# Order of VectorE's queue in the first batch of a Fourier and mixer kernel: weight sums first, two folds spread over more quarters

## The chip, the cores and the metric

The kernel runs on one core of one Trainium2 chip. The metric is the device time of one execution in microseconds (us). A difference of one to three us in 607 is at stake, so beside the times I use the traces: one profiled execution of each kernel, in which the start of every instruction can be read.

Engines: PE is TensorE (matmuls), PEld its weight loads, DVE is VectorE, ACT is ScalarE, POOL is GpSimd, SP is SyncE. In these traces VectorE works through its queue in the order in which the program issued its instructions; when the first one waits, those behind it wait too, ready or not (3.67 us of it are shown below).

## The reference, cut to what matters

```python
X = np.fft.fft(np.fft.fft(x, axis=1), axis=2)     # x: 8 batches of 3008 x 256
x = X.real
h  = np.maximum(x.transpose(0, 2, 1) @ w_tok1, 0) @ w_tok2
u  = x + h.transpose(0, 2, 1)
h2 = np.maximum(u @ w_ch1, 0) @ w_ch2
return u + h2
```

The real part of a two-dimensional Fourier transform of each batch is followed by a token mixer and a channel mixer.

## The kernel before: the parts that the change and the argument touch

The batches are pipelined. While batch b runs through its two channel products (`mm1`, `mm2`), pieces of the front part of batch b + 1 (transform and token mixer) and of the *fold* of batch b + 2 are strewn between them. x1 is the input of batch 1, fold one its fold, and so on. A batch has 24 *quarters* (`sub`): six columns of 512 tokens (`c`) in four steps (`s`). The fold is VectorE work: it adds mirrored rows, which a gather has brought into `xm`, to the rows in `xp`, and writes sums and differences of mirrored channels to `eo`. It has four groups of three pieces:

```python
def fold(b, engs):
    xp, xm = x_tiles.pop(b)
    eo = perb.tile([KR, NR, D], FP16, tag="eo", name="eo")
    for s, (t0, t1) in enumerate(((13, 17), (9, 13), (5, 9), (1, 5))):
        ...
        tt(out=xp[:, t, 1:D], in0=xp[:, t, 1:D], in1=xm[0:KR, rv, D - 1:0:-1], op=add)   # L457
        yield
        tt(out=eo[:, t, 1:129], in0=xp[:, t, 1:129], in1=xp[:, t, 255:127:-1], op=add)   # L461
        yield
        tt(out=eo[:, t, 129:256], ..., op=sub)                                           # L463
        yield
```

`xp`, `xm` and `eo` have one buffer each, so the load of x2 can start only when the last piece of fold one has read x1.

The second channel product takes seven block products in place of eight. It needs four sums of its weights once (`weight_sums`, L233 in the trace, read in batch 0 from quarter 9 on) and, for every column, sums of blocks of the activations (`block_sums`, L753):

```python
def weight_sums():                     # wc2 -> wst, four VectorE adds
    ...
def block_sums(c1, sb, k, which):      # c1 -> sb and in place in c1, VectorE
    ...
def mm2_sums(b, c, c1, s, box):        # per quarter: 24 small matmuls (L777) that read c1, sb, wc2, wst
    ...
    # L762 on VectorE and GpSimd: adds that empty PSUM into the output tile osb
```

The main loop of before, cut to the schedule:

```python
plan = [[0] * 10 + [2] * 14,  [1] * 13 + [0] + [2, 1] * 5]     # pieces of the front part of b + 1
fold_at = [15, 10]
for b in range(BB):
    nxt = front(b + 1) ...
    folds = fold(b + 2, ...)
    for c in range(NCH):
        for s in range(4):
            sub = 4 * c + s
            n = plan[b > 0][sub]
            mm1(b, c, c1, range(3 * s, 3 * s + 3))
            if s == 3: now()                  # block_sums
            take(own, ...); take(nxt, n // 2)
            if s == 0: now()
            mm2(*prev, s, pbox)
            if s == 2: now()
            ...
            take(nxt, n - n // 2)
            if s == 1: now()
            ...
            if b == 0 and sub == 4:
                weight_sums()
            if b == 0 and sub == 3:
                for h in range(2): swap_wc1(h)
            if b == 0 and 3 <= sub < 9:
                take(early, 2)                # early = fold(1)
                if sub == 8: x_tiles[2] = load_x(2)
            if folds is not None and sub >= fold_at[b > 0]:
                take(folds, 1 + (b == 0))
                ...                           # load_x(b + 3) after the last piece
```

## Time and profile before

| | before |
|---|---|
| time, median of 3 (lowest to highest) | 607.27 us (607.20 to 607.56) |
| span in the profile | 605.8 us |
| TensorE busy | 97% |
| listed TensorE waits in batch 0 (46 to 112 us) | 3.1 us |
| listed TensorE waits after 112 us | none |

From the page of before: busy time of each engine, and the shares of the chain of waits by engine.

```profile
PE 589.6 (97%) x6323; PEld 421.7 (70%) x6323; DVE 454.3 (75%) x1022; ACT 437.0 (72%) x983; POOL 148.5 (25%) x234
...
PE 86%; DMA 6%; DVE 5%; issue 1%; ACT 1%; POOL 1%; DVEq 0%; POOLq 0%
```

The list of TensorE's waits of before in 46 to 112 us (total, times, longest):

```profile
PE py L777 <- DVE sb L753: 1.7, 2, 1.2
PE pt L604 <- DVE w L590: 0.7, 1, 0.7
PE px L777 <- DVE osb L762: 0.5, 2, 0.2
PE px L777 <- DVE c L753: 0.2, 1, 0.2
```

Here `sb` and `c` are the block sums, `osb` is the output tile, and `w` is what the front part's transform hands to its token product (L604). From 46 us on TensorE is the limit, and all that it waits for is VectorE, in the first batch. Why VectorE is late shows in its timeline (start, duration, instruction, idle time before it and its releaser):

```profile
41.33 0.68 DVE L704 TENSOR_TENSOR ut<-pu,yt 128x512 f16<-128x512 f32 x1
45.68 0.23 DVE L455 TENSOR_TENSOR xp<-xp,xm 94x16 f16<-94x16 f16 x1 [3.67 <-DMA xm<-in_x_dram,ix]
...
47.12 0.68 DVE L704 TENSOR_TENSOR ut<-pu,yt 128x512 f16<-128x512 f32 x1
47.71 1.01 DVE L233 TENSOR_TENSOR wst<-wc 128x768 f16<-128x768 f16 x2
...
58.58 0.54 DVE L753 TENSOR_TENSOR sb<-c 128x768 f16<-128x768 f16 x1
59.16 0.56 DVE L753 TENSOR_TENSOR sb<-sb,c 128x768 f16<-128x768 f16 x1
...
80.60 1.21 DVE L455 TENSOR_TENSOR xp<-xp,xm 94x16 f16<-94x16 f16 x1
```

VectorE stops 3.67 us at the first piece of fold one, because the gather of x1 has not landed. The weight sums and an add for u (L704) stand behind that piece and could have run. From 45.7 us on VectorE works without a break, and the block sums `sb` of quarter 9 end at 59.7 us. TensorE wanted them earlier, as its timeline of the same stretch shows:

```profile
57.65 0.33 PE L777 MATMUL py<-wst,sb 128*128 128x128 f16 x3
59.18 0.68 PE L777 MATMUL py<-wst,sb 128*128 128x128 f16 x9 [1.20 <-DVE sb L753]
60.10 0.83 PE L777 MATMUL px<-wst,sb 128*128 128x128 f16 x12 [0.25 <-DVE osb L762]
60.77 1.46 PE L736 MATMUL pc<-ut,wc1p 128*128 128x512 f16 x6
```

The brackets add to 1.45 us. In what follows I use the **slip**: how much further apart the starts of two consecutive matmuls are than is usual (median) for such a pair in the same trace.

### The profile page before, as it was taken

The page shows a single profiled execution, that of the slowest core. Times are in us where ns is not written, and L with a number is a line of the kernel's source. Part 1 is how long each engine was busy: PE and PEld are TensorE (multiplying, and loading weights), DVE is VectorE, ACT ScalarE, POOL GpSimd, SP SyncE. Part 2 cuts the span into 40 slices and gives each one's busy share as a digit, 9 for nine tenths or more (in the row PEclk, how much of TensorE's full clock was granted, in tenths as well). Part 3 has the DMA queues.
Part 4 walks back from the last instruction along what each step waited for, and adds up shares of the span by engine and source line. Part 5 has one row for each costly group of instructions (what it writes and reads, how often), then busy time and mean ns, then how long its engine had stood idle before and what let it go on. Part 6 is the DMA issues. An engine that isn't in the chain of part 4 may idle for free.

```text
span 605.8 us, 15712 instructions
## 1 busy us (share of the span) xinstructions
PE 589.6 (97%) x6323; PEld 421.7 (70%) x6323; DVE 454.3 (75%) x1022; ACT 437.0 (72%) x983; POOL 148.5 (25%) x234
## 2 busy tenths in 40 slices
PE   5999999999999999999999999999999999999996
PEld 3855667666777677666777677766777677766675
DVE  8759699559886698667988689755979666766672
ACT  8775986777677767677767777677776877767772
POOL 7600414112242131402223211411221112111131
PEclk9999999999999999999999999999999999999999
DMA  9995945643457223662519332492231424242423
GB/s 152 210 177 117 176 62 97 141 62 63 53 107 155 57 54 88 134 88 54 97 44 178 70 80 63 83 173 53 54 85 44 86 53 88 55 70 62 87 60 99
DMA packets 86665, 56.53 MB, mean 93 GB/s; under 512 B 54928, under 2 KB 83536, under 8 KB 85840
## 3 DMA queue, kind: packets, MB, share of 16 engines
q1 hardware_dynamic: 78048, 37.84, 32.5%
q0 software_dynamic: 8320, 17.49, 16.9%
q8 instruction: 49, 0.80, 0.5%
q14 instruction: 24, 0.20, 0.1%
q10 hardware_dynamic: 224, 0.20, 0.1%
HBM read 34.98 MB, written 24.64 MB: 98 GB/s over the span
## 4 chain that ended last, share of the span: by engine, by line
PE 86%; DMA 6%; DVE 5%; issue 1%; ACT 1%; POOL 1%; DVEq 0%; POOLq 0%
PE pc L736 37%; PE px L777 23%; PE py L777 9%; PE pu L696 6%; PE po L834 3%; PE pt L604 3%; DMA xm<-in_x_dram,ix 3%; DMA w2s<-in_moe_w_tok_dram 2%; PE pz L509 1%; DMA w1p<-in_moe_w_tok_dram 1%; DVE sb L753 1%; PE pq L636 1%; PE py L636 1%; DVE osb L762 1%; DVE xp L457 1%
## 5 line engine op out<-in xcount | busy, mean ns | idle before, releaser
L739 ACT ACTIVATE c<-pc 128x512 f16<-128x512 f32 (+1 forms) x572 | 295.8, 593 | 38.2 <-PE pc L736 20.6
L762 POOL TENSOR_TENSOR osb<-osb,rt 128x256 f32<-128x256 f32 x84 | 81.2, 966 | 375.6 <-DVE osb L762 359.9
L736 PE MATMUL pc<-ut,wc1p 128*128 128x512 f16 x576 | 140.5, 379 | 0.0
L777 PEld LDWEIGHTS <-c 128*128 128x128 f16 x2016 | 121.4, 98 | 20.7 <-issue 1.3
L736 PE MATMUL pc<-ut,wc1m 128*128 128x512 f16 (+1 forms) x576 | 134.8, 370 | 0.0
L704 DVE TENSOR_TENSOR ut<-pu,yt 128x512 f16<-128x512 f32 (+1 forms) x96 | 64.7, 674 | 52.7 <-PE pu L696 52.7
L777 PEld LDWEIGHTS <-sb 128*128 128x128 f16 x1512 | 89.9, 98 | 12.5 <-DVE sb L753 2.1
L782 ACT ACTIVATE m<-px 128x256 f32<-128x256 f32 x126 | 48.6, 386 | 68.6 <-PE px L777 43.1
L736 PEld LDWEIGHTS <-wc1p 128*128 128x128 f16 x576 | 52.2, 98 | 49.1 <-issue 2.6
L736 PEld LDWEIGHTS <-wc1m 128*128 128x128 f16 x576 | 53.0, 98 | 46.4
L777 PE MATMUL px<-wst,c 128*128 128x128 f16 x1008 | 70.8, 219 | 0.2 <-DVE c L753 0.2
L777 PE MATMUL px<-wc,c 128*128 128x128 f16 x1008 | 63.1, 219 | 0.0
L753 DVE TENSOR_TENSOR sb<-sb,c 128x768 f16<-128x768 f16 x84 | 50.3, 599 | 2.9
L305 ACT ACTIVATE z<-pz 128x480 f16<-128x480 f32 (+1 forms) x60 | 40.0, 671 | 16.9 <-PE pz L509 11.0
L753 DVE TENSOR_TENSOR sb<-c 128x768 f16<-128x768 f16 x84 | 49.8, 592 | 2.3 <-ACT c L739 2.3
L762 DVE TENSOR_TENSOR osb<-py,m 128x256 f32<-128x256 f32 x84 | 35.2, 419 | 20.8 <-ACT m L782 18.9
L696 PE MATMUL pu<-w2p,uu 128*128 128x512 f16 (+1 forms) x168 | 50.0, 379 | 0.0
L753 DVE TENSOR_TENSOR sb<-c,sb 128x768 f16<-128x768 f16 x84 | 47.2, 561 | 0.0
L753 DVE TENSOR_TENSOR c<-c 128x768 f16<-128x768 f16 x84 | 46.6, 555 | 0.0
L590 DVE SCALAR_TENSOR_TENSOR w<-alt,pw 128x131 f16<-128x131 f16 x84 | 29.3, 350 | 18.2 <-ACT w L305 17.6
L643 DVE TENSOR_TENSOR yt<-py,qs 128x512 f16<-128x512 f32 x48 | 30.9, 686 | 15.7 <-ACT qs L639 14.8
L777 PE MATMUL py<-wst,sb 128*128 128x128 f16 x504 | 35.3, 219 | 1.7 <-DVE sb L753 1.7
(184 smaller groups left out, 681.0 us busy)
## 6 DMA issues: line engine op xcount, KB each, us to landing
out_dram<-osb SPq DMA_DIRECT2D x83, 256.0 KB, 3.7
xp<-in_x_dram POOLq DMA_DIRECT2D x16, 272.0 KB
out_dram<-osb SPq DMA_DIRECT2D x11, 192.0 KB, 3.2
xp<-in_x_dram POOLq DMA_DIRECT2D x16, 127.5 KB
rt<-ut SPq DMA_TRANSPOSE x96, 3.6
w2s<-in_moe_w_tok_dram POOLq DMA_DIRECT2D x1, 1504.0 KB
w1p<-in_moe_w_tok_dram POOLq DMA_DIRECT2D x4, 192.0 KB
wc<-in_moe_w_ch_dram POOLq DMA_DIRECT2D x1, 768.0 KB
```

What stands on the lines that cost most here:

```text
L305: nc.scalar.activation(out=out_, in_=in_, func=AFT.Copy)
L590: nc.vector.scalar_tensor_tensor(out=w[:, g, 0:131], in0=alt[:], scalar=pw[:, 131:132], in1=pw[:, 0:131], op0=AT.mult, op1=AT.add)
L604: nc.tensor.matmul(pt[:, o:o + n], lhsT=hw[:, g, th * P:th * P + P], rhs=w[:, g, f:f + n], start=(g == 0), stop=(g == NG - 1))
L643: nc.vector.tensor_tensor(out=yt[:, h, CW * c:CW * c + CW], in0=py[:], in1=qs[:], op=op)
L696: nc.tensor.matmul(pu[:, 0:n], lhsT=uu[:, th, int(minus), h, :], rhs=w2_cols(b, c)[:, th], start=(th == 0), stop=(th == 1))
L704: nc.vector.tensor_tensor(out=ut[:, h, 0:n].rearrange("p (a b) -> p a b", b=64), in0=pu[:, 0:n].rearrange("p (b a) -> p a b", b=64), in1=y ...
L736: nc.tensor.matmul(pc[:, 0:n], lhsT=wc[:, h, ct * P:(ct + 1) * P], rhs=ut[:, h, 0:n], start=(h == 0), stop=(h == 1))
L739: nc.scalar.activation(out=c1[:, ct, 0:n], in_=pc[:, 0:n], func=AFT.Relu)
L753: nc.vector.tensor_tensor(out=o, in0=x, in1=y, op=op)
L762: eng.tensor_tensor(out=o, in0=x, in1=y, op=AT.add)
L777: nc.tensor.matmul(o[:, t], lhsT=a(k)[:, f:f + P], rhs=w(k), start=(first and t == 0 and k == 0), stop=(k == HC - 1), skip_group_check=True)
L782: nc.scalar.activation(out=m[:, i], in_=pa[:, 0], func=AFT.Copy)
```

## The change

Its intent is to put VectorE's work in an order in which nothing that TensorE will soon need stands behind something that is early or blocked: the weight sums run while x1 is awaited; fold one is spread over quarters 4 to 10 in place of 3 to 8; fold two takes one piece a quarter from 15 on in place of two, and its last three pieces, with the load of x3, go to quarters 0 to 2 of batch 1. The front part's 28 pieces in batch 0 stay, but quarters 20 to 23 take 1, 2, 2, 3 of them in place of 2, 2, 2, 2.

```diff
-    plan = [[0] * 10 + [2] * 14,
-            [1] * 13 + [0] + [2, 1] * 5]
-    fold_at = [15, 10]
+    plan = [[0] * 10 + [2] * 10 + [1, 2, 2, 3]] + [[1] * 13 + [0] + [2, 1] * 5] * (BB - 1)
...
+    early_plan = [0] * 4 + [2, 2, 1, 2, 1, 2, 2] + [0] * 13
+    fold_plan = [[0] * 15 + [1] * 9] + [[0] * 10 + [1] * 12 + [0, 0]] * (BB - 1)
+    fold_plan[1] = [1, 1, 1] + fold_plan[1][3:]
...
-                if b == 0 and sub == 4:
+                if b == 0 and sub == 3:
                     weight_sums()
-                if b == 0 and sub == 3:
                     for h in range(2):
                         swap_wc1(h)
-                if b == 0 and 3 <= sub < 9:
-                    take(early, 2)
-                    if sub == 8:
+                if b == 0 and early_plan[sub]:
+                    take(early, early_plan[sub])
+                    if sub == 10:
                         x_tiles[2] = load_x(2)
-                if folds is not None and sub >= fold_at[b > 0]:
-                    take(folds, 1 + (b == 0))
-                    if sub == fold_at[b > 0] + (5 if b == 0 else 11) and b + 3 < BB:
+                if folds is not None and fold_plan[b][sub]:
+                    take(folds, 1)
+                    if b == 1 and sub == 2:
+                        x_tiles[3] = load_x(3)
+                        folds = fold(3, [nc.vector] * 4)
+                    elif sub == 21 and b and b + 3 < BB:
                         x_tiles[b + 3] = load_x(b + 3)
```

More of the change, by code (lines that the diff above doesn't have):

```diff
@@ L917 @@
     work = ctx.enter_context(tc.tile_pool(name="work", bufs=1))
-    plan = [[0] * 10 + [2] * 14,
-            [1] * 13 + [0] + [2, 1] * 5]
-    fold_at = [15, 10]
+    plan = [[0] * 10 + [2] * 10 + [1, 2, 2, 3]] + [[1] * 13 + [0] + [2, 1] * 5] * (BB - 1)
     own_plan = [[2, 1, 1, 1, 1, 1, 1, 0, 1, 1, 0, 0, 1, 1] + [0] * 10,
                 [1, 1, 1, 0, 0, 1, 1, 0, 1, 1, 0, 0, 1, 1] + [0] * 10]
+    own_plan += [[1, 1, 1, 0, 0, 1, 1, 0, 1, 1, 0, 0, 1, 1] + [0] * 10] * (BB - 2)
+    early_plan = [0] * 4 + [2, 2, 1, 2, 1, 2, 2] + [0] * 13
+    fold_plan = [[0] * 15 + [1] * 9] + [[0] * 10 + [1] * 12 + [0, 0]] * (BB - 1)
+    fold_plan[1] = [1, 1, 1] + fold_plan[1][3:]
     prev = None
@@ L929 @@
         nxt = front(b + 1) if b + 1 < BB else iter(())
-        folds = fold(b + 2, [nc.vector] * 4) if b + 2 < BB else None
+        if b != 1:
+            folds = fold(b + 2, [nc.vector] * 4) if b + 2 < BB else None
         for c in range(NCH):
@@ L939 @@
                 sub = 4 * c + s
-                n = plan[b > 0][sub]
+                n = plan[b][sub]
                 mm1(b, c, c1, range(3 * s, 3 * s + 3))
@@ L950 @@
                     now()
-                take(own, own_plan[b > 0][sub])
+                take(own, own_plan[b][sub])
                 take(nxt, n // 2)
```

## The prediction

> **What bounds the kernel now.** TensorE. The page shows it busy 97% of a 605.8 us span, clock full throughout; the chain of waits is 86% TensorE. From 112 us to the end its list of waits is empty, so nothing can be gained there. [...] All steady gaps are in batch 0 (46-112 us), each behind VectorE: 1.20 us waiting for block sums and 0.25 for an output add (58-60 us); 0.54, 0.25 and 0.17 us (83-88 us); 0.71 us for the last w column fix (93.8 us). Sum 3.1 us: the whole prize.
>
> **Why VectorE is late.** At 41.9 us it stops 3.7 us for the gathered half of x1, with the first fold piece at the head of its queue. The four weight sums (2.3 us) and one u add (0.6 us) stand behind it; from 45.6 us it is busy without a break until 60 us. From 76.5 to 95 us it is full again, as fold two puts all 12 pieces (0.4-0.7 us each) into six quarters. Two pieces beside a GpSimd add took 1.34 and 1.21 us (usual 0.41 and 0.22)[...].
>
> **What the change does.** It adds and removes no work. (1) Weight sums and that u add run in the 3.7 us hole: their weights were there by 42.5 us, when TensorE read them without waiting. VectorE is 2.9 us ahead after 45.6 us. (2) Fold one ends at quarter 10, not 8: about 1.3 us of pieces move behind the block sums that stopped TensorE at 58 us. Together about 4 us against a 1.45 us stall: it should vanish. (3) Fold two is halved between 80 and 94 us; three pieces go to batch 1, where VectorE idles 1.1 us at a time. The 0.17 and 0.71 us gaps should vanish.
>
> **What it costs.** x2 reuses x1's buffer, so its load starts only when fold one ends: I expect about 65.3 us instead of 61.6. Before, its transfers ended about 76.7 us, 15 us after issue; now about 80 us. TensorE being 1.5 us ahead, VectorE wants x2 at about 79.1 us. So a new wait of about 1 us for x2 at the head of VectorE's queue, of which I give 0.5-0.7 us to TensorE (the 0.54 and 0.25 us gaps largely stay). x3's load moves from 99.5 to about 116 us, its fold starts near 138 us: free. Front two needs the last part of fold two only at quarter 4 of batch 1: free.
>
> **Sum.** 3.1 us of gaps less 0.6 us left = 2.5 us. 607.3 - 2.5 = 604.8 us; 80% range 603.7 to 606.4. Faster by over 2%: 0.01; within 2%: 0.98; slower: 0.01.
>
> **What would show it.** VectorE's wait for x1 shrinks from 3.7 to about 1 us, weight sums start near 42 us; no TensorE wait at 55-60 us or for w near 92 us; x2's load issued near 65 us and a VectorE wait for it near 79-80 us; span 2-3 us shorter; still no TensorE wait in batches 1 to 7.
>
> **What would make it wrong.** x2 landing earlier (gain 3.1 us) or several us later, when block sums behind it stop TensorE (gain under 1.5 us); ScalarE, full from 62 to 73 us, becoming the next limit; new collisions of fold pieces with GpSimd adds; x3's load delaying GpSimd's adds and thereby the output stores.

## The result, and the profile after

| | before | changed |
|---|---|---|
| median (lowest to highest), 4 runs each | 607.24 us (606.57 to 607.56) | 605.41 us (605.11 to 605.55) |
| ratio, with 95% interval | | 0.9971 (0.9953 to 0.9988) |
| span in the profile | 605.8 us | 603.8 us |
| slips in batch 0 | 4.2 us | 1.8 us |

A ratio is the mean time of one kernel's fast runs over that of the other's of the same rounds, so it is not quite the ratio of the medians. The class is "same" at 2%; the interval excludes no difference. The predicted 604.8 us (603.7 to 606.4) holds the measured time.

From the page of the changed kernel:

```profile
PE 589.0 (98%) x6323; PEld 421.3 (70%) x6323; DVE 453.8 (75%) x1022; ACT 436.7 (72%) x983; POOL 146.0 (24%) x234
...
PE 93%; DVE 3%; ACT 3%; issue 0%; DVEq 0%; POOL 0%; POOLq 0%
```

The loads have left the chain of waits, and TensorE's share has grown from 86 to 93%. The list of TensorE's waits in 46 to 112 us has two lines left:

```profile
PE px L777 <- DVE c L753: 0.6, 1, 0.6
PE px L777 <- DVE osb L762: 0.5, 2, 0.3
```

VectorE's timeline at the places shown for before, and two later ones:

```profile
41.98 1.02 DVE L233 TENSOR_TENSOR wst<-wc 128x768 f16<-128x768 f16 x2
...
44.70 0.22 DVE L455 TENSOR_TENSOR xp<-xp,xm 94x16 f16<-94x16 f16 x1
...
55.34 0.55 DVE L753 TENSOR_TENSOR sb<-c 128x768 f16<-128x768 f16 x1
55.93 0.56 DVE L753 TENSOR_TENSOR sb<-sb,c 128x768 f16<-128x768 f16 x1
...
78.86 1.22 DVE L455 TENSOR_TENSOR xp<-xp,xm 94x16 f16<-94x16 f16 x1
...
97.72 1.29 DVE L643 TENSOR_TENSOR yt<-py,qs 128x512 f16<-128x512 f32 x2 [0.92 <-ACT qs L639]
98.93 0.55 DVE L753 TENSOR_TENSOR c<-c 128x768 f16<-128x768 f16 x1
```

The weight sums start where VectorE stood still before, the hole is gone, and the block sums of quarter 9 end at 56.5 us instead of 59.7. TensorE no longer stops there. It still stops for 0.25 us at 82.6 us, in quarter 17 as before, and at two later places, 90 and 99 us:

```profile
57.70 0.83 PE L777 MATMUL py<-wst,sb 128*128 128x128 f16 x12
58.37 0.83 PE L777 MATMUL px<-wst,sb 128*128 128x128 f16 x12
59.04 1.46 PE L736 MATMUL pc<-ut,wc1p 128*128 128x512 f16 x6
...
90.06 1.50 PE L777 MATMUL px<-wc,c 128*128 128x128 f16 x24 [0.28 <-DVE osb L762]
...
98.63 0.33 PE L777 MATMUL px<-wst,c 128*128 128x128 f16 x3
99.53 0.68 PE L777 MATMUL px<-wst,c 128*128 128x128 f16 x9 [0.57 <-DVE c L753]
```

Where the two us come from can be followed by the start of the first matmul of `mm1` in a quarter, counted from the start of quarter 0 of batch 0 (at 32.9 us in most traces). Quarters 21 to 23 are left out, because the change gives them other work.

| kernel (trace) | x1 landed, us | quarter 10 | quarter 18 | quarter 20 | batch 1, quarter 0 | last product |
|---|---|---|---|---|---|---|
| before | 45.1 | 27.86 | 52.71 | 58.11 | 73.70 | 562.96 |
| changed | 43.6 | 26.08 | 50.46 | 55.52 | 71.31 | 560.85 |
| a1_sums | 45.4 | 26.08 | 50.92 | 56.32 | 71.90 | 561.21 |
| a2_fold1 | 44.6 | 26.08 | 50.91 | 56.32 | 71.90 | 561.36 |
| a3_fold2 | 43.8 | 26.36 | 50.76 | 55.81 | 71.59 | 561.10 |
| a4_oldplan | 43.6 | 26.08 | 50.46 | 55.52 | 70.52 | 560.02 |
| after_again | 44.3 | 26.08 | 50.46 | 55.52 | 71.30 | 560.42 |
| b1_sums21 | 43.8 | 26.08 | 50.46 | 55.51 | 70.55 | 560.01 |
| b3_both | 44.7 | 26.08 | 49.79 | 54.85 | 70.03 | 559.47 |
| b4_old_moved | 44.5 | 26.08 | 49.79 | 54.85 | 69.99 | 559.36 |
| b5_start16 | 43.9 | 26.08 | 49.79 | 54.85 | 69.58 | 559.06 |
| d1_before_x1late | 46.5 | 28.71 | 55.19 | 60.59 | 76.18 | 565.65 |
| d2_after_x1late | 45.7 | 26.08 | 50.47 | 55.52 | 71.31 | 560.62 |

"x1 landed" is the end of the last packet of the queue that carries the loads issued by GpSimd, from the DMA records of the trace, counted from the start of the span. The changed kernel is 1.78 us ahead at quarter 10, 2.25 at quarter 18, 2.59 at quarter 20, 2.39 at the end of the batch and 2.1 at the last product. The last 0.3 us are no property of the change: they go mostly in slips of 0.1 us in batches 1 and 5, which this trace has and the one of before has not. A second trace of the changed kernel (after_again, below) has none of these, and its last product starts at 560.42. So the last column varies by some 0.4 us between executions of one kernel, and the gain at the end is 2.1 to 2.5 us by the traces.

One thing in the table needs an explanation. Up to quarter 3 the two programs are the same, yet x1 landed 1.5 us earlier in the trace of the changed kernel. Did the order remove the wait of quarter 9, or the early landing? The profiled pair cannot tell.

### The profile page after: what moved, and what is told of

Read it like the earlier page. It is cut to its first block, busy times and chain, and to the rows that moved or that the text cites. A ratio compares the mean times of both kernels' runs of the same rounds, so it can differ in the third digit from the quotient of the medians.

```text
span 603.8 us, 15712 instructions
## 1 busy us (share of the span) xinstructions
PE 589.0 (98%) x6323; PEld 421.3 (70%) x6323; DVE 453.8 (75%) x1022; ACT 436.7 (72%) x983; POOL 146.0 (24%) x234
## 3 DMA queue, kind: packets, MB, share of 16 engines
q1 hardware_dynamic: 78048, 37.84, 32.9%
## 4 chain that ended last, share of the span: by engine, by line
PE 93%; DVE 3%; ACT 3%; issue 0%; DVEq 0%; POOL 0%; POOLq 0%
PE pc L736 39%; PE px L777 23%; PE py L777 9%; PE pu L696 7%; PE po L834 4%; PE pt L604 4%; PE pz L509 1%; PE pq L636 1%; PE py L636 1%; PE pw L588 1%; PE pw L587 1%; DVE sb L753 1%; ACT c L739 0%; PE pw L551 0%; DVE osb L762 0%
## 5 line engine op out<-in xcount | busy, mean ns | idle before, releaser
L762 POOL TENSOR_TENSOR osb<-osb,rt 128x256 f32<-128x256 f32 x84 | 79.5, 946 | 367.7 <-DVE osb L762 360.6
L736 PEld LDWEIGHTS <-wc1m 128*128 128x128 f16 x576 | 52.9, 98 | 46.5
L753 DVE TENSOR_TENSOR sb<-c 128x768 f16<-128x768 f16 x84 | 47.4, 564 | 2.0 <-ACT c L739 2.0
L753 DVE TENSOR_TENSOR c<-c 128x768 f16<-128x768 f16 x84 | 46.5, 554 | 0.0
L590 DVE SCALAR_TENSOR_TENSOR w<-alt,pw 128x131 f16<-128x131 f16 x84 | 29.4, 351 | 18.1 <-ACT w L305 17.4
L643 DVE TENSOR_TENSOR yt<-py,qs 128x512 f16<-128x512 f32 x48 | 30.9, 686 | 15.7 <-ACT qs L639 14.9
```

What stands on the lines that cost most here:

```text
L590: nc.vector.scalar_tensor_tensor(out=w[:, g, 0:131], in0=alt[:], scalar=pw[:, 131:132], in1=pw[:, 0:131], op0=AT.mult, op1=AT.add)
L643: nc.vector.tensor_tensor(out=yt[:, h, CW * c:CW * c + CW], in0=py[:], in1=qs[:], op=op)
L736: nc.tensor.matmul(pc[:, 0:n], lhsT=wc[:, h, ct * P:(ct + 1) * P], rhs=ut[:, h, 0:n], start=(h == 0), stop=(h == 1))
L753: nc.vector.tensor_tensor(out=o, in0=x, in1=y, op=op)
L762: eng.tensor_tensor(out=o, in0=x, in1=y, op=AT.add)
```

## The experiments

**Undoing and doing parts.** Theory: the order of VectorE's queue is what counts, and either half of the first part would remove the slip at quarter 9. Rival: x1's landing decided it.

a1_sums is before with the weight sums first and nothing else:

```diff
-                if b == 0 and sub == 4:
+                if b == 0 and sub == 3:
                     weight_sums()
-                if b == 0 and sub == 3:
                     for h in range(2):
```

> The kernel before with one part of the change alone: the four weight sums ahead of fold one, which keeps its two pieces in each of quarters 3 to 8. Theory (VectorE's queue order): the sums fill the hole while x1 lands, VectorE is 2.3 to 2.9 us ahead, the waits at 58-60 us (1.20 and 0.25 us listed, 1.78 us by the slip of the matmul starts) vanish; the waits at 83-94 us stay. Gain 1.6 to 1.8 us, about 605.5. Rival (x1's landing moved: 45.1 us in the trace of before, 43.6 us in the changed kernel's, with the same program up to there): the gain follows the landing of x1 and not the order; then the wait at 58 us is 1 us or more whenever x1 lands at 45 us.

Measured: 605.98 us (605.84 to 607.00) against 606.42 us (605.86 to 607.24) for before on that chip; ratio 1.0000 (0.9986 to 1.0014). The trace is clear where the time is not: x1 landed at 45.4 us, later than in the trace of before, and the slip at quarter 9 is gone (26.08 in the table). So the order removes it, and the rival falls for this kernel. But the expected gain in time, 1.6 to 1.8 us, did not come: on this chip before itself ran between 605.9 and 607.2 us (the slowest with a mean clock of 0.995). The fastest of these runs are as fast as a1_sums, which has no slip at quarter 9. Whether they had none either is not shown, as they were not traced.

a2_fold1 is before with fold one spread alone:

```diff
+    early_plan = [0] * 3 + [2, 1, 1, 1, 2, 1, 2, 2] + [0] * 13
-                if b == 0 and 3 <= sub < 9:
-                    take(early, 2)
-                    if sub == 8:
+                if b == 0 and early_plan[sub]:
+                    take(early, early_plan[sub])
+                    if sub == 10:
```

> The kernel before with fold one spread over quarters 3 to 10 alone (sums still behind the first two pieces, x2's load at quarter 10). Theory: about 1.9 us of fold pieces move behind the block sums that stop TensorE at 58 us, so the 1.78 us slip there shrinks to 0-0.4 us; x2 is loaded about 3.5 us later and still lands (10 to 13 us after its issue near 65 us) before VectorE wants it at 79 us. Gain 1.3 to 1.8 us: either part alone would nearly do, and the gains of the two do not add. Rival (the hole is what matters): the slip at 58 us stays above 1 us and the gain is under 0.8 us.

Measured: 605.91 us (605.87 to 606.03), ratio 0.9994 (0.9981 to 1.0008). The slip at quarter 9 is gone here as well, with x1 at 44.6 us; the time again shows no gain outside the noise of before. Either half is enough by the traces, so their gains do not add.

a3_fold2 is the changed kernel with the sums and fold one put back: fold two, the load of x3 and the shifted plan alone.

```diff
-                if b == 0 and sub == 3:
+                if b == 0 and sub == 4:
                     weight_sums()
+                if b == 0 and sub == 3:
                     for h in range(2):
-    early_plan = [0] * 4 + [2, 2, 1, 2, 1, 2, 2] + [0] * 13
+    early_plan = [0] * 3 + [2] * 6 + [0] * 15
-                    if sub == 10:
+                    if sub == 8:
```

> The kernel before with the second half of the change alone: fold two at one piece a quarter, its last three pieces and x3's load in batch 1, and the shifted plan of front one. Fold one and the sums as before. Theory: the 1.78 us slip at 58-60 us stays; of the slips of 2.4 us at 83-94 us about 0.6 us goes (those for c and w go, two new ones of 0.4 and 0.7 us come at quarters 20 and 22). Gain 0.4 to 0.8 us, about 606.6. Rival: relief of VectorE at 80-94 us is the main gain, 1.5 us or more.

Measured: 605.68 us (605.51 to 605.73), ratio 0.9989 (0.9976 to 1.0003). The gain over before's median, 0.7 us, is as expected, though the interval does not exclude none. But the slip at quarter 9, expected to stay at 1.78 us, is 0.28. Its order up to there is that of before; only x1 landed at 43.8 us:

```profile
44.20 0.23 DVE L455 TENSOR_TENSOR xp<-xp,xm 94x16 f16<-94x16 f16 x1 [2.21 <-DMA xm<-in_x_dram,ix]
```

So in the old order the slip depends on the landing, which differs from run to run. With the sums first it does not arise at 43.6 us (changed) or 45.4 us (a1_sums). Both theories had a part of the truth.

a4_oldplan is the changed kernel with only the front part's plan put back:

```diff
-    plan = [[0] * 10 + [2] * 10 + [1, 2, 2, 3]] + ...
+    plan = [[0] * 10 + [2] * 14] + ...
```

> The changed kernel with only the shift of front one's pieces in quarters 20 to 23 undone (2, 2, 2, 2 instead of 1, 2, 2, 3). Theory: the slip of 0.74 us at quarter 22 (block sums c behind the two y adds) and the one of 0.42 us at quarter 20 are the price of the shift and go; in their place the last w column is late for the first token product by 0.2 to 0.9 us. Time within 0.5 us of the changed kernel, 604.9 to 605.6. Rival: the shift is what removed the wait for w and pays: without it 0.7 us or more slower.

Measured: 604.58 us (604.49 to 605.93), ratio 0.9977 (0.9964 to 0.9991): under the changed kernel's medians (605.41 and 605.31, on other chips) and under the expected range. The table, counted from quarter 0 of each trace, says the same: equal up to quarter 20, then 0.79 us less at the end of the batch. The slips of 0.42 and 0.74 us at quarters 20 and 22 are gone; one of 0.41 us for w came in their place:

```profile
90.60 0.22 PE L604 MATMUL pt<-w,hp 128*128 128x130 f16 x1 [0.24 <-DVE w L590]
```

The shifted plan is a loss of about 0.8 us inside the change.

**The changed kernel again, and mending what is left.** after_again is the changed kernel without an edit, in five rounds.

> The changed kernel itself, against the kernel before on one chip, in five rounds. Theory: before's wait at 58 us follows the landing of x1 (43.6 to 45.4 us in six profiled runs), so its times spread over 1 us or more and its mean gap to the changed kernel is smaller than the profiled pair's 2.0 us: 1.0 to 1.8 us; the changed kernel spreads under 0.5 us (605.1 to 605.6). Rival: a fixed gap of 2 us.

Measured: 605.31 us (605.25 to 606.21) against 606.78 us (606.18 to 607.67), ratio 0.9978 (0.9964 to 0.9991). The gap of medians is 1.5 us, within the expected 1.0 to 1.8; the spread is wider than the expected 0.5 us, by one run. Four of five runs of the changed kernel lie within 0.41 us, nine of before over 1.5 us. The fifth, 606.21 us, is the profiled one: its granted clock is 0.996 on average. Its trace shows half clock for 3.4 us at 15.8 us (matmuls of L426 took 0.42 us at 18.3 and 18.7 us, and 0.27 from 19.4 us on), and quarter 0 starts at 34.05 us instead of 32.9. This costs 1.15 us before any changed instruction, and explains why its span (604.4 us) is longer than that of the first profile (603.8 us). From quarter 0 to the end of batch 0 the table's figures are the same; the last product starts 0.4 us earlier. The clock does not explain the spread of before: its nine runs from 606.18 to 607.67 us all had a granted clock of 0.998 or more, the slowest 0.999.

b1_sums21 is the changed kernel with the block sums of quarter 21 issued first in that quarter. In the changed kernel they stand behind the two adds for y (L643, 1.29 us), which wait for ScalarE, as the lines at 97.72 and 98.93 us above show.

```diff
                 take(own, own_plan[b][sub])
+                if b == 0 and sub == 21:
+                    now()
                 take(nxt, n // 2)
...
-                if s == 1:
+                if s == 1 and (b, sub) != (0, 21):
                     now()
```

> The changed kernel with the block sums of quarter 21 issued before front one's pieces of that quarter, so that they no longer stand behind the two y adds of 1.29 us. Theory: the slip of 0.74 us of TensorE at quarter 22 (waiting for c) goes, the others (0.25, 0.41, 0.42 us) stay; 0.7 us under the changed kernel, about 604.6. Rival (the y adds then come late and stop the u matrices' products or ScalarE instead): the slip moves and the time stays within 0.2 us.

Measured: 604.48 us (604.47 to 604.64), ratio 0.9963 (0.9949 to 0.9976), 0.8 us under after_again. The slip of 0.74 us is gone, the other three (0.25, 0.41, 0.42) are unchanged, and no new one has come. The wait for `c` at quarter 22 was caused by the place of the y adds.

b3_both adds to this a later fold two, away from the quarters with a GpSimd add of the output beside it. b4_old_moved has the same fold two with the old plan in place of the moved block sums.

```diff
-    fold_plan = [[0] * 15 + [1] * 9] + ...
-    fold_plan[1] = [1, 1, 1] + fold_plan[1][3:]
+    fold_plan = [[0] * 17 + [1, 1, 0, 0, 2, 2, 0]] + ...
+    fold_plan[1] = [2, 2, 1, 1] + fold_plan[1][4:]
-                    take(folds, 1)
-                    if b == 1 and sub == 2:
+                    take(folds, fold_plan[b][sub])
+                    if b == 1 and sub == 3:
```

> As b1_sums21, and fold two starts at quarter 17 and keeps out of the quarters whose end or start has a GpSimd add of the output beside it: six pieces in batch 0 (quarters 17, 18, 21, 22), six in batch 1 (quarters 0 to 3), x3's load at quarter 3 of batch 1. Theory: the first piece no longer takes 1.2 us beside a GpSimd add, VectorE is on time at quarters 17 and 20, the slips of 0.25, 0.41 and 0.42 us go as well; about 1.8 us under the changed kernel, 603.5. Rival: the pieces moved to quarters 0 to 3 of batch 1 cause new waits there of 0.5 us or more.

> The changed kernel with the old plan of front one (as a4_oldplan, 604.6) and fold two moved as in b3_both. Theory: of a4_oldplan's slips (0.25 and 0.41 us at quarter 17, 0.40 us for w at quarter 20) all go; about 1.0 us under a4_oldplan, 603.5, the same as b3_both within 0.3 us. Rival: w is late for another reason than fold pieces (ScalarE's halves) and 0.4 us stays.

Measured: 603.96 us (603.95 to 604.27), ratio 0.9955 (0.9941 to 0.9968), and 603.99 us (603.85 to 604.07), ratio 0.9954 (0.9941 to 0.9968). In both the slips of 0.25 and 0.41 us at quarter 17 are gone, and the first instruction of fold two is short again. In the changed kernel GpSimd was at an add of the output at that moment:

```profile
78.82 1.16 POOL L762 TENSOR_TENSOR osb<-osb,rt 128x512 f32<-128x512 f32 x1 [6.64 <-DVE osb L762]
```

In b3_both it was idle:

```profile
84.73 0.22 DVE L455 TENSOR_TENSOR xp<-xp,xm 94x16 f16<-94x16 f16 x1
```

The instruction took 0.22 us instead of 1.22 us. In the traces of before and of the changed kernel, which have seven folds each, the first instruction of fold two is the only one of its kind that ran beside a GpSimd add, and took 1.21 and 1.22 us, ending 0.1 us after the add; the other six took 0.22 to 0.23 us. What slows it is not shown. The move also takes a piece out of each of quarters 15 and 16, so the collision is not isolated; but the 1.0 us that it added is more than the two slips together (0.66). The expected time was missed by 0.5 us, because a slip of 0.55 us stayed at quarter 20 in both (for `osb` in b3_both, for `w` in b4_old_moved). VectorE is busy from 83.8 to 90.1 us without a break in b3_both, and the pieces at quarters 17 and 18 fall into that stretch. No wait of TensorE is listed in batch 1.

b5_start16 is b4_old_moved with the first piece one quarter earlier, where VectorE had been idle:

```diff
-    fold_plan = [[0] * 17 + [1, 1, 0, 0, 2, 2, 0]] + ...
+    fold_plan = [[0] * 16 + [1, 0, 1, 0, 0, 2, 2, 0]] + ...
```

> As b4_old_moved, with fold two's first piece in quarter 16 instead of 17, where VectorE idles 0.54, 0.70 and 0.76 us in the trace of b3_both; the stretch from 83.8 to 90.1 us that is busy without a break loses 0.95 us. Theory: the last slip of 0.55 us at quarter 20 (for w) goes; 603.4 to 603.6, and no TensorE wait over 0.1 us in 46-112 us. Rival: the piece at quarter 16 meets a GpSimd add (0.67 us at 81.6 us), is slow as before, and the slip comes back at quarter 17: 603.9 to 604.2.

Measured: 603.66 us (603.51 to 604.84) against 606.68 us (606.30 to 607.32), ratio 0.9949 (0.9935 to 0.9962). The slip at quarter 20 shrank from 0.55 to 0.14 us, and the list of TensorE's waits from 40 us to the end is empty. As the rival said, the piece met a GpSimd add (0.67 us from 82.54 us) and was slow again:

```profile
82.58 0.71 DVE L455 TENSOR_TENSOR xp<-xp,xm 94x16 f16<-94x16 f16 x1
```

But no slip came back at quarter 17: here VectorE had the time. b5_start16 beats both kernels: 3.0 us under before, and 1.7 us under the changed kernel by the medians of different chips (1.4 and 1.8 by the last column of the table, for the two traces of the changed kernel). Its slowest run, 604.84 us, is the profiled one, with a mean granted clock of 0.997: 44.0 us of its span lie outside the table's stretch from quarter 0 to the last product (603.1 less 559.06), as in after_again (604.4 less 560.42), against 42.8 in b4_old_moved (602.2 less 559.36).

**The loads.** In d1_before_x1late and d2_after_x1late an extra load of 384 KB, which nobody reads, goes ahead of x1's on the same queue, in before and in the changed kernel.

```diff
     load_wc2()
+    pad = const.tile([P, 1536], FP16, tag="pad")
+    gdma(pad[:], dram(w2_t, 0, [[S, P], [1, 1536]]))
     if BB > 1:
         x_tiles[1] = load_x(1)
```

> The kernel before with an extra load of 384 KB into a tile nobody reads, on the same queue ahead of x1's, so that x1 lands some 1.8 us later (46 to 47 us). Theory: the slip of TensorE at 58-60 us follows x1's landing one for one once it is past 43.5 us (0.28 us at 43.8, 1.78 us at 45.1): 2.8 to 3.6 us now, time 607.8 to 608.6. Rival (the slip is set by the amount of VectorE's work and not by the landing): slip and time as before within 0.5 us.

> The changed kernel with the same extra load. Theory: VectorE waits about 1.5 to 2 us for x1 after the weight sums, but the sums are done and fold one is spread, so the block sums of quarter 9 are still on time: slip at 57-60 us under 0.3 us, time 605.2 to 605.8. So the change makes the kernel indifferent to x1's landing, and the gain against d1_before_x1late is 2.5 us or more. Rival: the changed kernel loses the 1.8 us too (607).

Measured: 609.26 us (608.40 to 610.66), ratio 1.0040 (1.0027 to 1.0054), and 605.25 us (605.13 to 606.55), ratio 0.9981 (0.9967 to 0.9994). The same extra load raises the median of the old order by 2.6 us and that of the new one not at all (605.41 and 605.31 us without it, on other chips); the two differ by 4.0 us. In the changed kernel VectorE did wait for x1, after the weight sums, and quarter 10 still starts at 26.08:

```profile
46.19 0.23 DVE L455 TENSOR_TENSOR xp<-xp,xm 94x16 f16<-94x16 f16 x1 [1.47 <-DMA xm<-in_x_dram,ix]
```

In the old order the slip follows the first fold piece. Counted from quarter 0, that piece starts at 11.31 us (a3_fold2), 12.78 (before) and 13.64 (d1_before_x1late), and the slip up to quarter 10 is 0.28, 1.78 and 2.63 us: in these three traces one for one. (The last is a little under the expected 2.8 to 3.6.)

d1_before_x1late was slower than the expected 607.8 to 608.6 us, and for its profiled run of 610.66 us a reason stands in the clock column. Here are two stretches of it (busy time of each engine, then PEclk, the granted TensorE clock, then DMA share and GB/s):

```profile
58.00:62.00 4.00, 1.89 (x26) 1.43 (x26) 3.96 (x9) 0.40 (x1) 0.67 (x1) 0.99 0.62 140
62.00:65.00 3.00, 3.00 (x15) 1.35 (x13) 2.05 (x4) 2.40 (x5) 2.30 (x5) 0.50 1.51 79
```

After waits of 0.20, 1.66 and 0.25 us, listed between 58 and 61.3 us with 12 short matmuls among them, the clock was halved for 3.4 us, and quarter 18 is 2.48 us behind before, though quarter 10 was only 0.85 behind: 1.6 us more. The other run over 610 us has the same mean clock, 0.997; the three with 0.999 took 608.40, 608.56 and 609.26 us. So the halved clock is not what puts the median, 609.26 us, 0.7 us above the range; that stays open.

c1_x2late asks for the other load: how much time x2 has.

```diff
-                    if sub == 10:
-                        x_tiles[2] = load_x(2)
+                if b == 0 and sub == 13:
+                    x_tiles[2] = load_x(2)
```

> The changed kernel with x2's load issued at the end of quarter 13 instead of 10, about 6 us later (71.5 us instead of 65.2). Theory: x2 has 2.8 us to spare in the changed kernel (landed 76.0 us, wanted 78.9 us), so it now lands at about 82.3 us, VectorE waits about 3.4 us at the head of its queue, and the block sums behind it stop TensorE for 2 to 3 us more: 607.3 to 608.3. Rival (TensorE has work enough in store): under 1 us slower than the changed kernel.

Measured: 616.90 us (616.50 to 619.62), ratio 1.0185 (1.0165 to 1.0204). This was far worse than expected. The load was issued at 69.8 us instead of 65.2, but landed at 89.1 us instead of 76.0:

```profile
89.59 0.23 DVE L455 TENSOR_TENSOR xp<-xp,xm 94x16 f16<-94x16 f16 x1 [10.70 <-DMA xm<-in_x_dram,ix]
```

TensorE lost 10.0 us to that one piece, and the clock was halved from 85.3 to 95.6 us, so the first 4 us of its work after the wait ran at half clock. The expectation that VectorE's wait for x2 becomes TensorE's wait was right. The assumption that the load keeps its length was wrong: from the first packet to the last it took 17.4 us instead of 9.5. That length is not peculiar to this run: x3's load, of the same size, took 15.7 us in the changed kernel and 9.4 in before. Between 73 and 77 us its queue moved little although hardly anything else moved either (10, 15, 39 and 85 GB/s over all queues in those four us, against 151 to 223 in the four before). Why is open. So in the changed kernel the load of x2 has 2.9 us to spare (landed 75.96, wanted 78.86), and in this run a shift of its issue by 4.7 us cost some 11 us.

## Why the prediction was right, and which of its steps were not

**Bound and size of the prize.** Right in kind: TensorE is the limit, its waits are all behind VectorE in batch 0, and batches 1 to 7 show no wait before or after. The 3.1 us of listed gaps were too small a figure for the prize. The slips of the same places add to 4.2 us, because a gap also breaks the overlap of matmuls (0.16 us in the traces: at quarter 9 the slips of 1.37 and 0.41 us are 0.17 and 0.16 more than the listed 1.20 and 0.25). The gaps were called steady as well; the one at quarter 9 is not: 0.28 us with x1 at 43.8 us and 1.78 us with x1 at 45.1 us.

**Weight sums in the hole, fold one spread.** Right: together they remove the slip at quarter 9 (57.70 and 58.37 us above, without brackets). Each alone does, too. VectorE's wait for x1 was expected to shrink to 1 us; it was 0 in this trace because x1 landed early, and 1.47 us in d2_after_x1late, where it cost TensorE nothing.

**Fold two halved.** The gaps for `c` at quarter 18 and for `w` at quarter 20 went, as said; but fold two halved did not do all of it for `w`: with the old plan (a4_oldplan) 0.41 of its 1.0 us stays, and the shifted plan takes that away. What the prediction failed to cost is the shifted plan: it puts the two y adds before the block sums of quarter 21, and a product before the token product of quarter 20, for slips of 0.74 and 0.42 us. a4_oldplan shows a net loss of 0.8 us, and b1_sums21 that the place of the block sums makes the larger slip.

**What it costs: x2.** Wrong. The load was issued at 65.16 us, as expected (65.3). But it took 10.8 us, not 15, and VectorE did not wait for it at all. The 15 us had been read from the end of all DMA traffic; the packets of the load itself had ended at 74.3 us in before, 12.7 us after issue. The gaps at quarter 17 did stay in part (slips of 0.25 and 0.41 us), as predicted, but not for x2. What fits is the first piece of fold two, which ran beside a GpSimd add; b3_both, which moves it, has neither slip.

**The sum.** Predicted gain 2.5 us: 3.1 us of gaps less 0.6 us left. By slips it was 4.2 less 1.8, so 2.4 us at the end of batch 0 and 2.1 at the last product, in this pair of traces. The times gave 1.8 and 1.5 us. The likely reason is that before's wait at quarter 9 is often shorter than in its profile; this is argued from a3_fold2 and d1_before_x1late, as before itself was traced once. That the predicted time held was in part luck: two errors of opposite sign nearly cancelled. The prize was taken 1.1 us too small, and 1.2 us of new slips from the plan were not seen. The 0.6 us put down to x2 had about the right size (0.66) for a wrong reason.

## What to carry to other kernels

On an engine that works in order, as VectorE did here (3.67 us behind a piece that was not ready), ask of every instruction at the head of the queue what stands behind it: work that is ready goes ahead of work that waits for a load, and work that another engine will soon need goes ahead of work for later. Before you take a gap of one profile as the prize, look whether it depends on when a load lands, and measure it from start to start of the waiting engine's instructions. If one part of a change moves several lists at once, undo each alone: here one of them took back 0.8 of the 3.2 us that the rest gains at the end of the first batch.

## What the traces show of the clock and of loads

- In d1_before_x1late the clock was halved for 3.4 us, to 65.3 us, after listed gaps that add to 2.1 us, the longest 1.66. In before, gaps of 1.20 and 0.25 us at the same place were followed by a full clock (1.00 from 57 to 64 us). In c1_x2late it was halved from 85.3 us, 3.7 us into a gap of 9.86 us, to 95.6 us. Whether the gaps bring it about, and from what length on, is not shown.
- The granted clock is first full at 10.7 us in the trace of before and at 9.5 us in that of the changed kernel. In after_again it was halved again for 3.4 us at about 15.8 us, which cost 1.15 us, more than half of what the change gains. Twelve other traces show nothing like it: ten have a mean clock of 0.999 or 1.000, and the means of d1_before_x1late (0.997) and c1_x2late (0.991) are used up by the halved stretches above. b5_start16 has 0.997 and loses 1.2 us outside the table's stretch.
- The landing of the same load varies: the queue that carries x1 ended between 43.6 and 45.4 us in the traces without the extra load. Why the load of x2, issued 4.7 us later, took 17.4 us instead of 9.5 from first to last packet is open.
- Listed TensorE gaps were too short: 3.1 us in batch 0 of before, against 4.2 us by the starts.
